# Retention feeding a softplus feed-forward layer: one 128x256 matmul per head in place of three 128x128, with the parts added in PSUM by VectorE

## The chip, the cores and the metric

The kernel runs on one core of a Trainium2 chip. The metric is device time in microseconds of one execution, as a median over several runs. TensorE does matrix products into PSUM, VectorE (DVE), ScalarE (ACT) and GpSimd (POOL) do elementwise work, and SyncE (SP) issues DMAs.

## The reference, cut to what matters

```python
gamma = 1.0 - 2.0 ** (-5.0 - np.arange(H))          # one decay per head; B, H, S, D = 4, 8, 768, 64
for t in range(S):
    state = gamma[None, :, None, None] * state + np.einsum('bhd,bhe->bhde', k[:, :, t], v[:, :, t])
    y[:, :, t] = scale * np.einsum('bhd,bhde->bhe', q[:, :, t], state)
...
x = y.transpose(0, 2, 1, 3).reshape(B * S, H * D)   # 3072 tokens of 512
h = x @ w_in                                        # 512 -> 2048, weights come as 64-bit floats
g = np.maximum(h, 0.0) + np.log1p(np.exp(-np.abs(h)))
return (g @ w_out).astype(np.float32)               # 2048 -> 512
```

## The kernel before, in words

The first layer is computed in chunks of 128 positions. A unit is one chunk of one batch entry and half of the heads (4 heads, in two pairs), so there are 24 x 2 = 48 units. Within a unit the output of a head is the sum of two products: v with the masked scores of this chunk, and the state carried from earlier chunks with q. The first chunk of a batch entry has no state.

From unit 10 on (`WHOLE = 10`) products run in the format fp32r, with each operand split into a high and a low part, and three of the four partial products are made: high-high, high-low, low-high. The first ten units use whole fp32 operands.

A unit passes through the steps `load_unit`, `decay`, `operands` (transposes of k and q into the PSUM tile `tp`, then the split into `kq`, and `vhl` with v's high and low part), `scores` (two PSUM tiles `sc`, one for each pair of heads, then `ah` and `al`, the scores' high and low part, each masked by a select on GpSimd), `new_state` (PSUM tile `pp`) and `stack_and_outputs` (state `st`, then PSUM tile `yp`, then the high and low part `xh`, `xl` of the layer's output). These steps are placed on ticks, four ticks a unit: `PARTS = {-6: load_unit, -2: decay, 0: operands, 2: scores, 3: new_state, 5: stack_and_outputs}`. `tp`, `sc`, `pp` and `yp` share one pool of three PSUM banks, `ps_a`; the other five banks hold `hp` (two), `acc` (two) and a tile for converting weights (`wp`).

The second and third products run on blocks of 256 tokens, in 8 steps a block. A step is `hidden` (24 matmuls into `hp`), softplus (VectorE L293, ScalarE L294, VectorE L298, ScalarE L300 `gh`, GpSimd L302 `gl`) and, two steps later, `second` (12 matmuls into `acc`). In the steady part, one tick is traced after `hidden` and one after `second`. A block's first step is traced two ticks after the outputs that it reads. The final order of each engine's instructions is chosen before the run by a planner that works with a model of times, so neighbouring steps can mix; on the chip each engine keeps that order.

In `outputs`, a head of a unit takes three matmuls of v with the scores (L249 to L251) and, where there is a state, two with q's high and low part (L242, L243), each with 64 weight columns and 128 moving columns, all summed in the one PSUM tile `yp`. Then ScalarE makes `xh` (L255) and VectorE `xl` (L257).

The tile `w` (L85, converted weights) has a pool `wts` of two slots of its own; `o` (L326, results on the way out) has two slots in the pool `ffn`.

Of the kernel before, what the change touches and what calls it, by code (L numbers as in the profile page):

```python
# [10 lines left out]
F32 = mybir.dt.float32  # L11
F32R = mybir.dt.float32r
I64 = mybir.dt.int64
U32 = mybir.dt.uint32
AF = mybir.ActivationFunctionType
ALU = mybir.AluOpType

P = 128
C = 128
# [3 lines left out]
WHOLE = 10  # L23
# [7 lines left out]
def decay_attention_then_softplus_ffn(ctx: ExitStack, tc: tile.TileContext, q, k, v, w_in, w_out, qtab, vtab, gtab, out):  # L31
    nc = tc.nc
    B, H, S, D = q.shape
    DM, DF = w_in.shape
# [4 lines left out]
    HH = H // 2  # L39
    NJ = HH // 2  # L40
# [2 lines left out]
    const = ctx.enter_context(tc.tile_pool(name="const", bufs=1))  # L43
    attn = ctx.enter_context(tc.tile_pool(name="attn", bufs=1))
    ffn = ctx.enter_context(tc.tile_pool(name="ffn", bufs=2))
    wts = ctx.enter_context(tc.tile_pool(name="wts", bufs=2))
    ps_h = ctx.enter_context(tc.tile_pool(name="ps_h", bufs=2, space=bass.MemoryType.PSUM))
    ps_o = ctx.enter_context(tc.tile_pool(name="ps_o", bufs=1, space=bass.MemoryType.PSUM))
    ps_w = ctx.enter_context(tc.tile_pool(name="ps_w", bufs=1, space=bass.MemoryType.PSUM))
    ps_a = ctx.enter_context(tc.tile_pool(name="ps_a", bufs=3, space=bass.MemoryType.PSUM))  # L50
# [23 lines left out]
    def convert_weights(f):  # L74

        n = ND * P
        converts[f] = []
        for nm, bits, to in zip(("win", "wout"), raw.pop(f), (win, wout)):
            words = bits.bitcast(U32).rearrange("p (n t) -> p n t", t=2)
            low, high = words[:, :, 0], words[:, :, 1]  # L80

            nc.scalar.activation(high.bitcast(F32), high.bitcast(F32), AF.Copy, scale=2.0**-112)

            wp = ps_w.tile([P, n], U32, name="wp")
            w = wts.tile([P, n], U32, name="w")  # L85

            nc.scalar.activation(wp, low, AF.Copy, scale=(1 - SLACK) * 2.0**-29, bias=7.5 * SLACK - 0.5)
            nc.vector.scalar_tensor_tensor(wp, high, 0x80000000, wp, op0=ALU.bitwise_and, op1=ALU.bitwise_or)
            nc.vector.scalar_tensor_tensor(w, high, 3, wp, op0=ALU.logical_shift_left, op1=ALU.bitwise_or)
            to[f] = const.tile([P, 2, n], F32R, name=f"{nm}hl", tag=f"{nm}{f}")  # L90
            converts[f].append(nc.scalar.copy(to[f][:, 0], w.bitcast(F32)).ins)
            nc.gpsimd.tensor_tensor(to[f][:, 1], w.bitcast(F32), to[f][:, 0].bitcast(F32), op=ALU.subtract)
# [4 lines left out]
    lo, up = slice(0, D), slice(D, P)  # L97
# [58 lines left out]
    def scores(n):  # L156
        kq = live[n][0]
        if n < WHOLE:
            kw, qw = kq
            parts = [attn.tile([P, HH, C], F32, name="ah")]  # L160
            sc = ps_a.tile([P, HH, C], F32, name="sc", tag="a")
            for h in range(HH):
                nc.tensor.matmul(sc[:, h, :], lhsT=kw[:, h // 2, :], rhs=qw[:, h % 2, h // 2, :], start=True, stop=True)
            nc.scalar.copy(parts[0], sc)
        else:
            parts = [attn.tile([P, HH, C], F32R, name=nm) for nm in ("ah", "al")]
            for j in range(NJ):

                sc = ps_a.tile([P, 2, 2, C], F32, name="sc", tag="a")
                for par in range(2):  # L170
                    nc.tensor.matmul(sc[:, par], lhsT=kq[:, 0, par, j, :], rhs=kq[:, 1:, par, j, :], start=True, stop=True)  # L171
                hi, low = (t[:, 2 * j:2 * j + 2, :] for t in parts)
                nc.scalar.copy(hi, sc[:, :, 0, :])
                nc.vector.tensor_tensor(low, sc[:, :, 0, :], hi.bitcast(F32), op=ALU.subtract)
                nc.vector.tensor_tensor(low, sc[:, :, 1, :], low.bitcast(F32), op=ALU.add)
        for t in parts:
            nc.gpsimd.affine_select(
                t, t.bitcast(F32), pattern=[[0, HH], [1, C]], compare_op=ALU.is_ge, fill=0.0, base=0, channel_multiplier=-1
            )
        live[n] += parts  # L180

# [45 lines left out]
    def outputs(n):  # L227
        b, c, hf = units[n]
        kq, *rest, st = live.pop(n)
        i, off = divmod((n // 2) * C, T)  # L230
        if i not in xs:
            xs[i] = [ffn.tile([P, ND, T], F32R, name=nm) for nm in ("xh", "xl")]
        xh, xl = xs[i]
        yp = ps_a.tile([D, 2, NJ, C], F32, name="yp", tag="a")
        for j in range(NJ):
            for par in range(2):
                h = 2 * j + par
                o = yp[:, par, j, :]
                if c and n < WHOLE:
                    nc.tensor.matmul(o, lhsT=st[:, j, :], rhs=kq[1][:, par, j, :], start=True, stop=False)  # L240
                elif c:
                    nc.tensor.matmul(o, lhsT=st[:, par, j, :], rhs=kq[:, 1, par, j, :], start=True, stop=False)  # L242
                    nc.tensor.matmul(o, lhsT=st[:, par, j, :], rhs=kq[:, 2, par, j, :], start=False, stop=False)  # L243
                if n < WHOLE:
                    kn, vn, a = rest
                    nc.tensor.matmul(o, lhsT=vn[:, h, :], rhs=a[:, h, :], start=c == 0, stop=True)  # L246
                else:
                    vhl, kh, kl, ah, al = rest
                    nc.tensor.matmul(o, lhsT=vhl[:, h, 0, :], rhs=ah[:, h, :], start=c == 0, stop=False)  # L249
                    nc.tensor.matmul(o, lhsT=vhl[:, h, 0, :], rhs=al[:, h, :], start=False, stop=False)  # L250
                    nc.tensor.matmul(o, lhsT=vhl[:, h, 1, :], rhs=ah[:, h, :], start=False, stop=True)  # L251
        g = hf * NJ
        to = [(par, x[rows, g:g + NJ, off:off + C]) for x in (xh, xl) for par, rows in ((0, lo), (1, up))]
        for par, hi in to[:2]:
            nc.scalar.copy(hi, yp[:, par])  # L255
        for (par, low), (_, hi) in zip(to[2:], to[:2]):
            nc.vector.tensor_tensor(low, yp[:, par], hi.bitcast(F32), op=ALU.subtract)  # L257

    def stack_and_outputs(n):
        stack_state(n)  # L260
# [1 line left out]


    PARTS = {-6: load_unit, -2: decay, 0: operands, 2: scores, 3: new_state, 5: stack_and_outputs}
    FIRST_TICK = min(PARTS)
    PERIOD = 4
# [38 lines left out]
    def second(s):  # L305
        i, p = steps[s]
        gh, gl = gs.pop(s)
        begins = s == 0 or steps[s - 1][0] != i
        ends = s + 1 == len(steps) or steps[s + 1][0] != i
        if begins:  # L310
            acc[i] = [ps_o.tile([P, DM], F32, name=f"acc{t}") for t in range(NT)]
        for k in range(2):
            wt = wout[2 * p + k]
            for t in range(NT):
                ts = slice(t * P, (t + 1) * P)
                nc.tensor.matmul(acc[i][t], lhsT=gh[:, k, ts], rhs=wt[:, 0], start=begins and k == 0, stop=False)  # L316
                nc.tensor.matmul(acc[i][t], lhsT=gh[:, k, ts], rhs=wt[:, 1], start=False, stop=False)  # L317
                nc.tensor.matmul(acc[i][t], lhsT=gl[:, k, ts], rhs=wt[:, 0], start=False, stop=ends and k == 1)  # L318
        if not ends:
            return  # L320
        for t in range(NT):
            if p < NP - 1:
                part[i, t] = ffn.tile([P, DM], F32, name="part")
                (nc.scalar.copy if t % 2 else nc.vector.tensor_copy)(part[i, t], acc[i][t])
                continue
            o = ffn.tile([P, DM], F32, name="o")  # L326
            if (i, t) in part:
                nc.vector.tensor_tensor(o, acc[i][t], part.pop((i, t)), op=ALU.add)
            else:
                (nc.scalar.copy if t % 2 else nc.vector.tensor_copy)(o, acc[i][t])  # L330
            nc.sync.dma_start(out[i * T + t * P:i * T + (t + 1) * P, :], o)
# [13 lines left out]
    def convert_to(n):  # L345
        nonlocal loaded, converted
        while converted < min(NF, n):
            convert_weights(converted)
            converted += 1
            if loaded < NF:  # L350
                load_weights(loaded)
                loaded += 1
# [30 lines left out]
    for a, b in zip(starts, starts[1:]):  # L383
        i = steps[b][0]
        if i == 2:
            a = b - TURN
# [4 lines left out]
    def stages(s, until):  # L391

        nonlocal done
        ok = lambda t: 0 <= t < len(steps)
        if ok(s):
            hidden(s)
            softplus_1(s)
            softplus_2(s)
        until = max(until, done)
        half = (done + until + 1) // 2  # L400
        while done < half:
            tick(done)
            done += 1
        if ok(s - LAG):
            second(s - LAG)
        while done < until:
            tick(done)
            done += 1
# [37 lines left out]
```

## Time and profile before

| | |
|---|---|
| median of 3 runs | 700.75 us (699.87 to 701.68) |
| the profiled execution | 700.03 us, span 698.2 us |
| busy: TensorE, its weight loads | 684.4, 621.3 us |
| busy: VectorE, ScalarE, GpSimd | 433.2, 372.1, 281.4 us |
| granted TensorE clock | 1.00 |

The span is the time from the first to the last instruction. Busy times of matmuls overlap one another, as matmuls are pipelined, so the cost of one is better read from the distance between starts. A row of a group gives line, engine, operation, tiles (written <- read), shape and count, then busy us and mean ns of one, then the engine's idle time ahead of it and what ended that.

### The profile page before, as it was taken

The page shows a single profiled execution, that of the slowest core. Times are in us where ns is not written, and L with a number is a line of the kernel's source. Part 1 is how long each engine was busy: PE and PEld are TensorE (multiplying, and loading weights), DVE is VectorE, ACT ScalarE, POOL GpSimd, SP SyncE. Part 2 cuts the span into 40 slices and gives each one's busy share as a digit, 9 for nine tenths or more (in the row PEclk, how much of TensorE's full clock was granted, in tenths as well). Part 3 has the DMA queues.
Part 4 walks back from the last instruction along what each step waited for, and adds up shares of the span by engine and source line. Part 5 has one row for each costly group of instructions (what it writes and reads, how often), then busy time and mean ns, then how long its engine had stood idle before and what let it go on. Part 6 is the DMA issues. An engine that isn't in the chain of part 4 may idle for free.

```text
span 698.2 us, 13537 instructions
## 1 busy us (share of the span) xinstructions
PE 684.4 (98%) x5056; PEld 621.3 (89%) x5056; DVE 433.2 (62%) x893; ACT 372.1 (53%) x835; POOL 281.4 (40%) x324
## 2 busy tenths in 40 slices
PE   6899999999999999999999999999999999999997
PEld 4688889899999999999999999999999999999996
DVE  4676785557666766557667666647766676544221
ACT  6988885446556546445555555445555544543221
POOL 5676667334343342343334333433433333222221
PEclk9999999999999999999999999999999999999999
DMA  9976650122112112111111111211211110000000
GB/s 266 287 201 173 192 159 1 31 61 69 31 23 69 31 25 61 31 31 54 39 23 37 49 38 24 61 37 25 62 24 39 54 31 16 31 1 1 31 1 30
DMA packets 90752, 42.82 MB, mean 61 GB/s; under 512 B 77376, under 2 KB 85568, under 8 KB 90688
## 3 DMA queue, kind: packets, MB, share of 16 engines
q1 hardware_dynamic: 90240, 41.96, 22.2%
q8 instruction: 40, 0.66, 0.4%
q14 instruction: 24, 0.20, 0.1%
q10 hardware_dynamic: 448, 0.01, 0.0%
HBM read 35.66 MB, written 6.29 MB: 60 GB/s over the span
## 4 chain that ended last, share of the span: by engine, by line
PE 96%; ACT 1%; issue 0%; DVE 0%; ACTq 0%
PE hp L286 14%; PE hp L287 13%; PE hp L288 13%; PE acc L316 13%; PE acc L317 13%; PE acc L318 13%; PE sc L171 3%; PE tp L125 1%; PE tp L127 1%; PE pp L195 1%; PE yp L250 1%; PE yp L251 1%; PE yp L249 1%; PE yp L246 1%; PE yp L240 1%; PE yp L243 1%
## 5 line engine op out<-in xcount | busy, mean ns | idle before, releaser
L286 PE MATMUL hp<-xh,winhl 128*128 128x256 f32 x768 | 221.4, 289 | 0.4 <-ACT xh L255 0.4
L288 PE MATMUL hp<-xh,winhl 128*128 128x256 f32 x768 | 217.9, 284 | 0.0
L287 PE MATMUL hp<-xl,winhl 128*128 128x256 f32 x768 | 217.6, 283 | 0.0
L302 POOL TENSOR_TENSOR gl<-sp,gh 128x512 fp32r<-128x512 f32 x96 | 125.4, 1306 | 149.3 <-ACT gh L300 86.7
L316 PE MATMUL acc<-wouthl,gh 128*128 128x512 f32 x384 | 154.3, 402 | 0.0
L317 PE MATMUL acc<-wouthl,gh 128*128 128x512 f32 x384 | 150.4, 392 | 0.0
L318 PE MATMUL acc<-wouthl,gl 128*128 128x512 f32 x384 | 149.1, 390 | 0.0
L286 PEld LDWEIGHTS hp<-xh,winhl 128*128 128x128 f32 x768 | 146.5, 191 | 2.8 <-issue 0.5
L287 PEld LDWEIGHTS hp<-xl,winhl 128*128 128x128 f32 x768 | 147.0, 191 | 1.6 <-issue 0.5
L288 PEld LDWEIGHTS hp<-xh,winhl 128*128 128x128 f32 x768 | 146.8, 191 | 0.6 <-issue 0.3
L293 DVE TENSOR_SCALAR sp<-hp 128x512 uint32<-128x512 uint32 x96 | 66.1, 690 | 70.6 <-PE hp L288 61.0
L300 ACT CAST gh<-sp 128x512 fp32r<-128x512 f32 x96 | 59.5, 620 | 74.1 <-PE acc L317 57.4
L117 POOL TENSOR_TENSOR qn<-qn,qtabs 128x256 f32<-128x256 f32 x48 | 29.4, 613 | 151.1 <-DMA qn<-in_q_dram 125.0
L294 ACT ACTIVATE sp<-sp 128x512 f32<-128x512 f32 x96 | 60.9, 634 | 49.0 <-DVE sp L293 48.7
L318 PEld LDWEIGHTS acc<-wouthl,gl 128*128 128x128 f32 x384 | 71.9, 188 | 15.6
L316 PEld LDWEIGHTS acc<-wouthl,gh 128*128 128x128 f32 x384 | 72.4, 189 | 12.5 <-issue 0.5
L317 PEld LDWEIGHTS acc<-wouthl,gh 128*128 128x128 f32 x384 | 72.5, 189 | 11.4
L298 DVE SCALAR_TENSOR_TENSOR sp<-hp,sp 128x512 f32<-128x512 f32 x96 | 65.9, 687 | 12.8 <-ACT sp L294 11.6
L142 DVE TENSOR_TENSOR kq<-tp,kq 64x256 fp32r<-64x256 f32 x76 | 32.1, 422 | 67.0 <-ACT kq L140 65.8
L139 ACT CAST kq<-tp 64x512 fp32r<-64x512 f32 x76 | 44.1, 581 | 40.0 <-PE tp L127 38.8
L255 ACT CAST xh<-yp 64x256 fp32r<-64x256 f32 x96 | 35.1, 366 | 51.0 <-PE yp L251 44.5
L257 DVE TENSOR_TENSOR xl<-yp,xh 64x256 fp32r<-64x256 f32 x96 | 39.9, 416 | 33.7 <-ACT xh L255 32.7
(85 smaller groups left out, 1082.6 us busy)
## 6 DMA issues: line engine op xcount, KB each, us to landing
win<-in_moe_w_in_dram SPq DMA_DIRECT2D x16, 512.0 KB, 4.5
wout<-in_moe_w_out_dram SPq DMA_DIRECT2D x16, 512.0 KB, 4.4
kn<-in_k_dram SPq DMA_DIRECT2D x48, 128.0 KB, 2.3
qn<-in_q_dram SPq DMA_DIRECT2D x48, 128.0 KB, 2.8
vn<-in_v_dram SPq DMA_DIRECT2D x48, 128.0 KB, 2.2
out_dram<-o SPq DMA_DIRECT2D x24, 256.0 KB, 2.1
gtab_sb<-in_gtab_dram ACTq DMA_DIRECT2D x2, 2.0 KB, 3.8
qtabs<-in_qtab_dram ACTq DMA_DIRECT2D x1, 4.0 KB, 2.4
```

What stands on the lines that cost most here:

```text
L139: nc.scalar.copy(kq[own, :2, par], tp[own])
L286: nc.tensor.matmul(hp[:, k], lhsT=wt[:, 0, d, :], rhs=xh[:, d, :], start=d == 0, stop=False)
L287: nc.tensor.matmul(hp[:, k], lhsT=wt[:, 0, d, :], rhs=xl[:, d, :], start=False, stop=False)
L288: nc.tensor.matmul(hp[:, k], lhsT=wt[:, 1, d, :], rhs=xh[:, d, :], start=False, stop=d == ND - 1)
L293: nc.vector.tensor_scalar(sp.bitcast(U32), hps[s].bitcast(U32), 0x80000000, None, op0=ALU.bitwise_or)
L294: nc.scalar.activation(sp, sp, AF.Softplus)
L298: nc.vector.scalar_tensor_tensor(g, hps.pop(s), 0.0, g, op0=ALU.max, op1=ALU.add)
L300: nc.scalar.copy(gh, g)
L302: nc.gpsimd.tensor_tensor(gl, sps.pop(s), gh.bitcast(F32), op=ALU.subtract)
L316: nc.tensor.matmul(acc[i][t], lhsT=gh[:, k, ts], rhs=wt[:, 0], start=begins and k == 0, stop=False)
L317: nc.tensor.matmul(acc[i][t], lhsT=gh[:, k, ts], rhs=wt[:, 1], start=False, stop=False)
L318: nc.tensor.matmul(acc[i][t], lhsT=gl[:, k, ts], rhs=wt[:, 0], start=False, stop=ends and k == 1)
```

## The change

The scores' two parts go into one tile `ahl` with the parts side by side for each head, masked by one select over both. In `outputs`, v's high and low part (128 weight columns) are multiplied with both parts of the scores (256 moving columns) in one matmul a head. It writes four fields: partitions 0 to 63 hold v-high with scores-high and, beside it, v-high with scores-low; partitions 64 to 127 hold v-low with scores-high and v-low with scores-low, and the last is not read. The matmuls with the state add into the first field. Then, for each of the two heads-in-pair positions, ScalarE copies the v-low field to partitions 0 to 63 of an SBUF tile `cross`, VectorE adds the v-high-scores-low field to it, and VectorE adds `cross` into the first field in PSUM. `xh` and `xl` are made from that field as before. `yp` is now one PSUM bank for each of the two positions, so two a unit. The first ten units keep their form. The pool `wts` goes; `w` shares the two slots of `o`.

```diff
-    wts = ctx.enter_context(tc.tile_pool(name="wts", bufs=2))
...
-            w = wts.tile([P, n], U32, name="w")
+            w = ffn.tile([P, n], U32, name="w", tag="o")
...
-            parts = [attn.tile([P, HH, C], F32R, name=nm) for nm in ("ah", "al")]
+            ahl = attn.tile([P, HH, 2, C], F32R, name="ahl", tag="ahl")
+            parts = [ahl]
...
-                hi, low = (t[:, 2 * j:2 * j + 2, :] for t in parts)
+                hi, low = (ahl[:, 2 * j:2 * j + 2, t, :] for t in range(2))
...
+            t = t if n < WHOLE else t.rearrange("p h t c -> p (h t) c")
             nc.gpsimd.affine_select(
-                t, t.bitcast(F32), pattern=[[0, HH], [1, C]], compare_op=ALU.is_ge, fill=0.0, base=0, channel_multiplier=-1
+                t, t.bitcast(F32), pattern=[[0, t.shape[1]], [1, C]], compare_op=ALU.is_ge, fill=0.0, base=0, channel_multiplier=-1
             )
...
-                    vhl, kh, kl, ah, al = rest
-                    nc.tensor.matmul(o, lhsT=vhl[:, h, 0, :], rhs=ah[:, h, :], start=c == 0, stop=False)
-                    nc.tensor.matmul(o, lhsT=vhl[:, h, 0, :], rhs=al[:, h, :], start=False, stop=False)
-                    nc.tensor.matmul(o, lhsT=vhl[:, h, 1, :], rhs=ah[:, h, :], start=False, stop=True)
...
+            vhl, kh, kl, ahl = rest
+            ys = []
             for par in range(2):
+                yp = ps_a.tile([P, NJ, 2, C], F32, name="yp", tag="a")
+                for j in range(NJ):
+                    h = 2 * j + par
+                    nc.tensor.matmul(yp[:, j], lhsT=vhl[:, h], rhs=ahl[:, h], start=True, stop=True)
+                    if c:
+                        o = yp[lo, j, 0, :]
+                        nc.tensor.matmul(o, lhsT=st[:, par, j, :], rhs=kq[:, 1, par, j, :], start=False, stop=False, skip_group_check=True)
+                        nc.tensor.matmul(o, lhsT=st[:, par, j, :], rhs=kq[:, 2, par, j, :], start=False, stop=True, skip_group_check=True)
+                cross = attn.tile([D, NJ, C], F32, name="cross", bufs=2)
+                nc.scalar.copy(cross, yp[up, :, 0, :])
+                nc.vector.tensor_tensor(cross, yp[lo, :, 1, :], cross, op=ALU.add)
+                nc.vector.tensor_tensor(yp[lo, :, 0, :], yp[lo, :, 0, :], cross, op=ALU.add)
+                ys.append(yp[lo, :, 0, :])
+        for y, (hi, low) in zip(ys, to):
+            nc.scalar.copy(hi, y)
+        for y, (hi, low) in zip(ys, to):
+            nc.vector.tensor_tensor(low, y, hi.bitcast(F32), op=ALU.subtract)
```

More of the change, by code (lines that the diff above doesn't have):

```diff
@@ L159, in scores @@
             kw, qw = kq
-            parts = [attn.tile([P, HH, C], F32, name="ah")]
+            parts = [attn.tile([P, HH, C], F32, name="ah", tag="ahl")]
             sc = ps_a.tile([P, HH, C], F32, name="sc", tag="a")
@@ L233, in outputs @@
         xh, xl = xs[i]
-        yp = ps_a.tile([D, 2, NJ, C], F32, name="yp", tag="a")
-        for j in range(NJ):
-            for par in range(2):
[L237 to L247, printed above, removed]
-                    vhl, kh, kl, ah, al = rest
-                    nc.tensor.matmul(o, lhsT=vhl[:, h, 0, :], rhs=ah[:, h, :], start=c == 0, stop=False)
-                    nc.tensor.matmul(o, lhsT=vhl[:, h, 0, :], rhs=al[:, h, :], start=False, stop=False)
-                    nc.tensor.matmul(o, lhsT=vhl[:, h, 1, :], rhs=ah[:, h, :], start=False, stop=True)
@@ L252, in outputs @@
[L252 to L257, printed above, removed]
+        g = hf * NJ
+        to = [[x[rows, g:g + NJ, off:off + C] for x in (xh, xl)] for rows in (lo, up)]
+        if n < WHOLE:
+            kn, vn, a = rest
+            yp = ps_a.tile([D, 2, NJ, C], F32, name="yp", tag="a")
+            for j in range(NJ):
+                for par in range(2):
+                    o = yp[:, par, j, :]
+                    if c:
+                        nc.tensor.matmul(o, lhsT=st[:, j, :], rhs=kq[1][:, par, j, :], start=True, stop=False)
+                    nc.tensor.matmul(o, lhsT=vn[:, 2 * j + par, :], rhs=a[:, 2 * j + par, :], start=c == 0, stop=True)
+            ys = [yp[:, par] for par in range(2)]
+        else:
+            vhl, kh, kl, ahl = rest
+            ys = []
+            for par in range(2):
+                yp = ps_a.tile([P, NJ, 2, C], F32, name="yp", tag="a")
+                for j in range(NJ):
+                    h = 2 * j + par
+                    nc.tensor.matmul(yp[:, j], lhsT=vhl[:, h], rhs=ahl[:, h], start=True, stop=True)
+                    if c:
+                        o = yp[lo, j, 0, :]
[6 more added lines that the diff above has]
+                ys.append(yp[lo, :, 0, :])
@@ L325, in second @@
                 continue
-            o = ffn.tile([P, DM], F32, name="o")
+            o = ffn.tile([P, DM], F32, name="o", tag="o")
             if (i, t) in part:
```

## The prediction

> **What bounds the kernel now.** I read the page's busy times first, then the windows by stage, then the waits of TensorE, and last the order in time around one group of v-times-score products.
>
> ```profile
> PE 684.4 (98%) x5056; PEld 621.3 (89%) x5056; DVE 433.2 (62%) x893; ACT 372.1 (53%) x835; POOL 281.4 (40%) x324
> ```
>
> ```profile
> 28.00:136.00 108.00, 108.00 (x748) 94.58 (x747) 74.01 (x126) 81.96 (x168) 69.27 (x69) 1.00 0.49 139
> ...
> 150.00:640.00 490.00, 490.00 (x3746) 451.72 (x3746) 321.83 (x693) 249.68 (x587) 178.35 (x208) 1.00 0.14 37
> ```
>
> The columns of the window rows are the stretch, its length, busy time of PE, PEld, DVE, ACT and POOL with counts, the granted clock, and the DMA share and rate. TensorE is busy in every one of the 490 us of the stage that the change touches, at a granted clock of 1.00, and VectorE in 322 of them (66%). The waits of TensorE, asked for the whole span, are a handful, all small and nearly all in the opening part; the last of them on the new code's path is this one:
>
> ```profile
> PE hp L286 <- ACT xh L255: 0.4, 1, 0.4
> ```
>
> So time comes off only where TensorE's own stream gets shorter, and goes on where TensorE gets a wait that it does not have now. A busy TensorE says little on what one matmul costs, since records overlap (0.22 us long, one every 0.06 us). I therefore price matmuls by the distance from one start to the next. One unit without a carried state (first column start, second duration):
>
> ```profile
> 333.25 0.39 PE L316 MATMUL acc<-wouthl,gh 128*128 128x512 f32 x1
> 333.48 0.39 PE L317 MATMUL acc<-wouthl,gh 128*128 128x512 f32 x1
> ...
> 333.93 0.22 PE L249 MATMUL yp<-ah,vhl 128*64 128x128 f32 x1
> 333.99 0.22 PE L250 MATMUL yp<-al,vhl 128*64 128x128 f32 x1
> ...
> 334.59 0.22 PE L251 MATMUL yp<-ah,vhl 128*64 128x128 f32 x1
> 334.65 0.33 PE L286 MATMUL hp<-xh,winhl 128*128 128x256 f32 x1
> 334.82 0.28 PE L287 MATMUL hp<-xl,winhl 128*128 128x256 f32 x1
> 334.94 0.28 PE L288 MATMUL hp<-xh,winhl 128*128 128x256 f32 x1
> ```
>
> Twelve yp matmuls of 128 moving columns take 334.65 - 333.93 = 0.72, so 0.06 each. An hp matmul of 256 columns takes 0.12, but the first after the yp group takes 0.17. An acc matmul of 512 takes 0.23. The weight loads tell where the extra 0.05 comes from:
>
> ```profile
> 334.53 0.13 PEld L251 LDWEIGHTS yp<-ah,vhl 128*64 128x64 f32 x1
> 334.59 0.19 PEld L286 LDWEIGHTS hp<-xh,winhl 128*128 128x128 f32 x1
> 334.70 0.19 PEld L287 LDWEIGHTS hp<-xl,winhl 128*128 128x128 f32 x1
> ...
> 340.86 0.14 PEld L195 LDWEIGHTS pp<-vhl,kh 128*64 128x64 f32 x1
> 340.92 0.14 PEld L196 LDWEIGHTS pp<-vhl,kl 128*64 128x64 f32 x1
> ```
>
> A load begins when the matmul ahead of its own begins (L286's load at 334.59 with L251's matmul at 334.59), so one load is ahead, not more. The load of 128 weight columns holds the next one off for 0.11, a load of 64 for 0.06. The pitch is thus the longer of two things: streaming this matmul's columns, or loading the next one's weights. After a yp matmul (0.06 of streaming) a load of 128 columns (0.11) shows as 0.05 lost.
>
> **The change part by part.** The form with high and low parts is used from unit 10 on:
>
> ```profile
> L249 PE MATMUL yp<-ah,vhl 128*64 128x128 f32 x152 | 33.2, 223 | 0.0
> L242 PE MATMUL yp<-kq,st 128*64 128x128 f32 x128 | 28.4, 222 | 0.0
> L171 PE MATMUL sc<-kq 128*128 128x256 f32 x152 | 25.3, 283 | 0.0
> ```
>
> 152 heads are 38 units; 128 of them have a state, so 32 units have one and 6 have none.
>
> *TensorE, the 6 units without a state.* Removed: 12 matmuls at 0.06, and the 0.05 on the following hp: 0.77. Added: 4 matmuls of 256 columns with 128 weight columns, the shape of L171, whose tile below shows four in 352.00 - 351.51 = 0.49, 0.12 each: 0.48. The next hp's load hides under 0.12. Gain 0.29 x 6 = 1.7 us.
>
> *TensorE, the 32 units with a state.* Removed: 20 x 0.06 + 0.05 = 1.25. After: for each head one wide matmul (0.12, the load of 64 columns hides under it), the first state matmul (0.06), the second state matmul, behind which a load of 128 columns must run (0.11, not 0.06). That is 0.29 a head, 1.16 a unit. Gain 0.09 x 32 = 2.9 us. Here nearly all of the three-to-one saving goes: the head has 3 matmuls for 5, but the wide weights are loaded behind a matmul too short to hide them.
>
> TensorE's sum is -4.6 us. Its bounds: at the good end every load hides, then each unit saves 0.29 and the sum is -11.0. At the bad end a wide load behind a state matmul costs what it costs behind pp's 64-column matmul, where the next hp takes 0.20 in place of 0.12:
>
> ```profile
> 341.21 0.19 PE L196 MATMUL pp<-vhl,kl 128*64 128x64 f32 x1
> 341.24 0.36 PE L286 MATMUL hp<-xh,winhl 128*128 128x256 f32 x1
> 341.44 0.28 PE L287 MATMUL hp<-xl,winhl 128*128 128x256 f32 x1
> ```
>
> Then a unit with state takes 4 x (0.12 + 0.06 + 0.06 + 0.08) = 1.28, loses 0.03, and the sum is +1.0 - 1.7 = -0.7. I take -4.6, since L286 behind L251 has the very shapes: 128 moving columns, then 128 weight columns.
>
> The Trainium skill speaks against this change too: TensorE: Matmul & The Clock Gate, section LDWEIGHTS, gives a load as weight columns over 1.2, so 107 ns for 128. By it a state unit takes 4 x (0.12 + 0.06 + 0.107) = 1.15 and the sum would be -4.9; the rows agree with it.
>
> *ScalarE and VectorE.* Added per unit, for each of two halves: a ScalarE copy of 64x256 out of PSUM (cross), a VectorE add of PSUM and SBUF into SBUF, and a VectorE add of PSUM and SBUF into PSUM. Prices by these rows:
>
> ```profile
> L140 ACT CAST kq<-tp 64x256 fp32r<-64x256 f32 x76 | 27.9, 367 | 0.9
> L202 DVE TENSOR_TENSOR td<-pp,td 64x256 f32<-64x256 f32 x32 | 13.3, 414 | 16.7 <-PE pp L196 15.7 <-PE pp L191 0.9
> L88 DVE SCALAR_TENSOR_TENSOR wp<-win,wp 128x512 uint32<-128x512 uint32 x16 | 11.1, 694 | 10.1 <-ACT wp L87 10.1
> L89 DVE SCALAR_TENSOR_TENSOR w<-win,wp 128x512 uint32<-128x512 uint32 x16 | 11.0, 685 | 0.9
> ```
>
> L88 writes PSUM and L89 SBUF, 694 against 685 ns, so an output in PSUM costs nothing to speak of. ScalarE gets 2 x 0.37 x 38 = 28 us, VectorE 4 x 0.414 x 38 = 63 us, to 496 of some 695 us, and about 380 of the 490 us stage (78%). Neither becomes the bound as a whole. Their cost is in latency only; what hides it is below.
>
> ```profile
> 347.39 0.22 PE L242 MATMUL yp<-kq,st 128*64 128x128 f32 x1
> ...
> 348.13 0.43 DVE L143 TENSOR_TENSOR kq<-tp,kq 64x256 fp32r<-64x256 f32 x1
> 348.59 0.69 DVE L298 SCALAR_TENSOR_TENSOR sp<-hp,sp 128x512 f32<-128x512 f32 x1
> 350.36 0.85 DVE L257 TENSOR_TENSOR xl<-yp,xh 64x256 fp32r<-64x256 f32 x2 [1.08 <-ACT xh L255]
> 351.23 0.43 DVE L147 TENSOR_TENSOR vhl<-vn,vhl 128x256 fp32r<-128x256 f32 x1
> 351.79 0.69 DVE L293 TENSOR_SCALAR sp<-hp 128x512 uint32<-128x512 uint32 x1
> ...
> 351.51 0.64 PE L171 MATMUL sc<-kq 128*128 128x256 f32 x4
> 352.00 0.40 PE L316 MATMUL acc<-wouthl,gh 128*128 128x512 f32 x1
> ```
>
> This unit's yp group runs from 347.39 for 20 x 0.06, to 348.59. VectorE has 1.08 idle ahead of xl; the adds are 1.66. So L293 starts some 0.6 later, and with it softplus, whose gh is read two steps later: covered. xl ends up to 1 us later than 351.20. A block's first hidden matmuls come behind 24 hp (2.9), 4 sc (0.5), 12 acc (2.7) and the pp matmuls after the last unit of the block: over 6 us against a chain of under 4. Covered.
>
> *PSUM banks.* Each unit now takes two banks of the pool of three for yp, not one. tp holds the third until L143 ends (348.56). The first sc tile can have tp's bank; the second needs the first yp tile's, free when its xl has been made. That is the one new wait on TensorE, and the acc matmuls are queued behind it. VectorE's shortest way there is 348.56 + 0.69 + 4 x 0.414 + 0.42 = 351.33, with the gaps of some 0.02 between instructions about 351.45; the second sc tile is wanted at 351.51 + 0.24 - 0.09 = 351.66. So it passes by 0.2, at nothing. Bounds: nothing, or 0.3 a unit (rival below). Below nothing it cannot be, as TensorE does not wait there now.
>
> *POOL.* Two selects of 128x512 become one of 128x1024, behind the later of the two parts. It costs at most twice 0.634 = 1.27:
>
> ```profile
> L177 POOL TENSOR_SCALAR_AFFINE_SELECT al<-al x38: 629/634/819, 132.6 to 636.5; 128x512 fp32r<-128x512 f32 x38
> ```
>
> The yp matmuls that read it come three ticks after sc, with at least 12 acc matmuls (2.7) or 24 hp (2.9) between ticks, and POOL is busy 178 of 490 us: nothing.
>
> *w in the slots of o.* Two slots as before, and the last w is written at 117.9 us, the first o at 140.4: nothing.
>
> ```profile
> L89 DVE SCALAR_TENSOR_TENSOR w<-wout,wp x16: 678/687/691, 12.5 to 117.9; 128x512 uint32<-128x512 uint32 x16
> ...
> L330 DVE COPY o<-acc x11: 678/680/692, 140.4 to 693.4; 128x512 f32<-128x512 f32 x11
> ```
>
> No DMA is added, removed or moved past anything.
>
> *The last unit* has no ticks behind it:
>
> ```profile
> 644.42 0.85 DVE L257 TENSOR_TENSOR xl<-yp,xh 64x256 fp32r<-64x256 f32 x2 [2.57 <-ACT xh L255]
> ...
> 646.96 0.28 PE L286 MATMUL hp<-xh,winhl 128*128 128x256 f32 x1
> ```
>
> Its xl ends at 645.27, VectorE idle ahead of it. One half's cross and two adds (0.37 + 2 x 0.41), which stay in its chain, take it to near 646.5, still ahead of the hp matmuls that read it, which come behind 12 acc. Nothing.
>
> The sum is -4.6. The profiled execution took 700.03 (span 698.2), 0.7 below the median of 700.75; against the median it is 696.1.
>
> **The rivals.**
>
> *A: as summed.* TensorE saves 2.2 to 7, no wait: 694 to 698.5 with 696.1 likeliest.
>
> *B: all loads hide.* 700.75 - 11.0 = 689.7. It needs a wide load that begins two matmuls ahead; against it, L286's load begins no earlier than L251's matmul. The Trainium skill, same page, section The mechanism, says that TensorE's queue pulls a load ahead of matmuls in flight where it goes to the background weights; by it this rival would come out; the trace shows one matmul ahead and no more.
>
> *C: part is given back.* The second sc tile waits about 0.1 a unit, 38 x 0.1 = 3.8: 699.9, no change to be told. For it: a margin of only 0.2. Against it: instructions are put in an order beforehand, and acc matmuls can be put ahead of sc.
>
> *D: the wait on the yp bank decides; slower.* If VectorE takes vhl (0.43) ahead of xl, the first yp tile comes free at 351.9 and TensorE stands 0.3 in each unit: 38 x 0.3 = 11.4, and 700.75 - 4.6 + 11.4 = 707.5. It decides from 4.6 / 38 = 0.12 a unit on. For it: vhl belongs to the unit's operands, traced ahead of the outputs. Against it: vhl comes last now although VectorE idles 1.08 ahead of xl.
>
> **How the numbers follow.** A 0.56, B 0.08, C 0.20, D 0.16. Within 0.3% (2.1 us, about what can be told from no change) lies C alone. Faster 0.64, same 0.20, slower 0.16. The range 691 to 703.5 leaves out B and most of D.
>
> **What would show it.** TensorE, by starts: 0.12 for the wide matmul, 0.06 and 0.11 for the two state matmuls; wide loads beginning with the second state matmul. Units without state: four at 0.12. VectorE near 496 us and ScalarE near 400. TensorE's waits: no row of sc on xl. Wrong it is if sc L171's second tile waits for VectorE by over 0.1 a unit, or if state matmuls are 0.06 throughout.

## The result and the profile after

The changed kernel takes 724.1 us as a median against 700.6 for the kernel before: ratio 1.033, interval 1.028 to 1.038. The forecast was 696.1, range 691.0 to 703.5. The four executions lie between 720.5 and 726.8; the profiled one is the longest of them, 726.77 us (span 725.0, so 26.8 more than before's 698.2).

The page's busy times, and the window of the middle stage (same columns as before: stretch, length, PE, PEld, DVE, ACT, POOL with counts, granted clock, DMA):

```profile
PE 694.9 (96%) x4752; PEld 631.6 (87%) x4752; DVE 472.8 (65%) x1045; ACT 398.1 (55%) x911; POOL 273.6 (38%) x286
```

```profile
150.00:640.00 490.00, 473.50 (x3300) 437.35 (x3299) 340.92 (x798) 262.79 (x631) 164.35 (x167) 0.98 0.14 37
```

Two things are new. TensorE, busy for all 490 us before, now stands still for 16.5 of them. And the granted clock, 1.00 before, is 0.98. The list of TensorE's waits names two causes that the kernel before did not have:

```profile
PE sc L172 <- DVE kq L142: 8.6, 9, 1.4
PE hp L298 <- DVE sp L310: 8.2, 10, 0.9
```

The columns are total us, times, longest. Nine waits for `kq` and ten for softplus's second VectorE instruction (one of them, 0.3 us, in the opening part): one pair for each block of the middle part, since a block takes about 58 us there and the stage is some 490. None is on `xl`, the tile whose lateness the prediction's rivals turned on.

The saving in TensorE's own stream is there, to the price. One yp group with a state, TensorE and its weight loads:

```profile
391.92 0.28 PE L256 MATMUL yp<-ahl,vhl 128*128 128x256 f32 x1
392.04 0.22 PE L259 MATMUL yp<-kq,st 128*64 128x128 f32 x1
392.10 0.22 PE L260 MATMUL yp<-kq,st 128*64 128x128 f32 x1
392.16 0.33 PE L256 MATMUL yp<-ahl,vhl 128*128 128x256 f32 x1
392.33 0.22 PE L259 MATMUL yp<-kq,st 128*64 128x128 f32 x1
392.39 0.22 PE L260 MATMUL yp<-kq,st 128*64 128x128 f32 x1
392.45 0.33 PE L256 MATMUL yp<-ahl,vhl 128*128 128x256 f32 x1
```

```profile
392.39 0.19 PEld L256 LDWEIGHTS yp<-ahl,vhl 128*128 128x128 f32 x1
392.50 0.14 PEld L259 LDWEIGHTS yp<-kq,st 128*64 128x64 f32 x1
```

The first wide matmul takes 0.12 to the next start, the state matmuls 0.06 each, and the second wide one 0.17. The extra 0.05 comes from the load of the wide weights. The load rows show it for the third wide matmul (392.45): its load begins with the state matmul ahead of it (L260 at 392.39) and holds the next load off for 0.11, to 392.50. That is 0.29 a head, as summed, so the forecast saving of 4.6 us in the stream stands. The other 31 us, by which the profiled execution is longer in spite of it, must lie in what TensorE waits for and in its clock.

**Where one pair of waits comes from.** The stretch around 392 us, in order of time (start, duration, engine, instruction; idle time ahead of it in brackets):

```profile
386.42 0.40 PE L172 MATMUL sc<-kq 128*128 128x256 f32 x2
388.88 0.41 DVE L176 TENSOR_TENSOR ahl<-sc,ahl 128x256 fp32r<-128x256 f32 x1
389.45 0.38 PE L124 MATMUL tp<-ident,kn 128*128 128x128 f32 x2
391.66 0.37 ACT L139 CAST kq<-tp 64x256 fp32r<-64x256 f32 x1
391.93 0.63 ACT L306 ACTIVATE sp<-sp 128x512 f32<-128x512 f32 x1
392.06 0.42 DVE L141 TENSOR_TENSOR kq<-tp,kq 64x256 fp32r<-64x256 f32 x1 [1.36 <-ACT kq L139]
393.36 0.43 DVE L142 TENSOR_TENSOR kq<-tp,kq 64x256 fp32r<-64x256 f32 x1
393.82 0.69 DVE L305 TENSOR_SCALAR sp<-hp 128x512 uint32<-128x512 uint32 x1
393.94 0.47 PE L172 MATMUL sc<-kq 128*128 128x256 f32 x2 [0.74 <-DVE kq L142]
394.54 0.69 DVE L310 SCALAR_TENSOR_TENSOR sp<-hp,sp 128x512 f32<-128x512 f32 x1
395.29 0.39 PE L298 MATMUL hp<-xh,winhl 128*128 128x256 f32 x1 [0.88 <-DVE sp L310]
```

Read it backwards. hp at 395.29 needs the hp bank that L310 frees. L310 is late since VectorE had to do four kq subtracts (L141 and L142, twice each) and L305 first. sc at 393.94 waits for the last of these subtracts. Before, kq had 12 acc, the yp and 24 hp matmuls of cover between `tp` (the row below, from the kernel before) and `sc` at 351.51, 7.3 us; here `sc` comes 4.5 us behind `tp`, right behind the yp matmuls, with no acc between. The missing acc matmuls are the mark of these places. In the middle part the changed kernel has nine units with no acc between `tp` and the first `sc` tile and 4.5 us from one to the other, and all nine wait; its other units have at least 12 acc there and 6.7 us or more, and none waits for kq. In all the other runs below, too, the first `sc` tile waits for kq only where no acc stands between (17 or 18 hp matmuls, 3.3 to 4.5 us).

```profile
344.19 0.38 PE L125 MATMUL tp<-ident,kn 128*128 128x128 f32 x2
```

In the changed kernel `tp` starts at 389.45, just after L176 (388.88 to 389.29) has read the previous unit's second `sc` tile for the last time. That tile's matmuls had come late in their turn (386.42).

**The clock.** In seven stretches of 3.4 us the granted clock was half. The first and the last of seven windows:

```profile
222.50:225.90 3.40, 3.40 (x19) 3.40 (x18) 2.47 (x7) 1.49 (x4) 2.12 (x3) 0.50 0.17 39
...
628.60:632.00 3.40, 3.32 (x15) 3.32 (x16) 2.94 (x9) 1.95 (x5) 1.95 (x2) 0.51 0.00 0
```

```profile
396.60 0.42 PE L299 MATMUL hp<-xl,winhl 128*128 128x256 f32 x1
396.82 0.42 PE L300 MATMUL hp<-xh,winhl 128*128 128x256 f32 x1
```

hp matmuls are 0.22 apart there, not 0.12. Each stretch begins within 1.4 us of the end of a pair of waits (seven of the nine pairs) and costs about 3.41 x (1 - 0.12 / 0.22) = 1.55 us, all seven 11. An eighth, at 24.5 us in the opening part, belongs to no such pair; the profiled execution before has none there, so it adds 1.5. The nine pairs of waits cost 2.0 to 2.6 each by start distances (0.9 to 1.5 at `sc`, 1.0 at hp), 18 to 20 us. With -4.6 that makes +26 to +28, against +26.8 measured. The four executions had granted clocks of 0.981 to 0.991, which is some eight to four half-clock stretches each: the median, 724.1, has fewer than the profiled execution.

### The profile page after: what moved, and what is told of

It reads as the page before. It is cut to its first block, busy times and chain, and to the rows that moved or that the text cites. A ratio compares the mean times of both kernels' runs of the same rounds, so it can differ in the third digit from the quotient of the medians.

```text
span 725.0 us, 13053 instructions
## 1 busy us (share of the span) xinstructions
PE 694.9 (96%) x4752; PEld 631.6 (87%) x4752; DVE 472.8 (65%) x1045; ACT 398.1 (55%) x911; POOL 273.6 (38%) x286
## 4 chain that ended last, share of the span: by engine, by line
PE 89%; DVE 4%; ACT 3%; issue 1%; DMA 0%; POOL 0%; POOLq 0%; DVEq 0%; ACTq 0%
PE hp L298 13%; PE acc L328 12%; PE hp L299 12%; PE hp L300 12%; PE acc L329 12%; PE acc L330 12%; PE yp L256 3%; PE sc L172 2%; PE tp L124 1%; PE pp L197 1%; PE tp L126 1%; PE yp L246 1%; PE sc L162 1%; PE yp L245 1%; ACT kq L138 1%; DVE sp L310 1%
## 5 line engine op out<-in xcount | busy, mean ns | idle before, releaser
L298 PE MATMUL hp<-xh,winhl 128*128 128x256 f32 x768 | 222.3, 292 | 8.6 <-DVE sp L310 8.2
L299 PE MATMUL hp<-xl,winhl 128*128 128x256 f32 x768 | 224.5, 292 | 0.0
L300 PE MATMUL hp<-xh,winhl 128*128 128x256 f32 x768 | 222.6, 290 | 0.0
L314 POOL TENSOR_TENSOR gl<-sp,gh 128x512 fp32r<-128x512 f32 x96 | 123.9, 1291 | 215.7 <-ACT gh L312 180.0
L298 PEld LDWEIGHTS hp<-xh,winhl 128*128 128x128 f32 x768 | 150.5, 197 | 14.9 <-DVE sp L310 9.7
L299 PEld LDWEIGHTS hp<-xl,winhl 128*128 128x128 f32 x768 | 151.3, 197 | 3.5 <-issue 0.5
L300 PEld LDWEIGHTS hp<-xh,winhl 128*128 128x128 f32 x768 | 151.5, 197 | 0.5 <-issue 0.2
L305 DVE TENSOR_SCALAR sp<-hp 128x512 uint32<-128x512 uint32 x96 | 65.8, 687 | 56.7 <-PE hp L300 53.3
L310 DVE SCALAR_TENSOR_TENSOR sp<-hp,sp 128x512 f32<-128x512 f32 x96 | 66.1, 688 | 11.0 <-ACT sp L306 9.1
L179 POOL TENSOR_SCALAR_AFFINE_SELECT ahl<-ahl 128x1024 fp32r<-128x1024 f32 x38 | 42.2, 1111 | 63.3 <-DVE ahl L176 50.4
L117 POOL TENSOR_TENSOR vn<-vn,vtabs 128x256 f32<-128x256 f32 x48 | 29.5, 615 | 87.2 <-DMA vn<-in_v_dram 47.2
L263 DVE TENSOR_TENSOR cross<-yp,cross 64x256 f32<-64x256 f32 x76 | 30.6, 409 | 43.5 <-ACT cross L262 43.4
L175 DVE TENSOR_TENSOR ahl<-sc,ahl 128x256 fp32r<-128x256 f32 x76 | 31.2, 411 | 36.0 <-ACT ahl L174 35.9
```

The lines of the kernel that those rows point to most:

```text
L179: nc.gpsimd.affine_select(t, t.bitcast(F32), pattern=[[0, t.shape[1]], [1, C]], compare_op=ALU.is_ge, fill=0.0, base=0, channel_multiplier=-1)
L298: nc.tensor.matmul(hp[:, k], lhsT=wt[:, 0, d, :], rhs=xh[:, d, :], start=d == 0, stop=False)
L299: nc.tensor.matmul(hp[:, k], lhsT=wt[:, 0, d, :], rhs=xl[:, d, :], start=False, stop=False)
L300: nc.tensor.matmul(hp[:, k], lhsT=wt[:, 1, d, :], rhs=xh[:, d, :], start=False, stop=d == ND - 1)
L305: nc.vector.tensor_scalar(sp.bitcast(U32), hps[s].bitcast(U32), 0x80000000, None, op0=ALU.bitwise_or)
L310: nc.vector.scalar_tensor_tensor(g, hps.pop(s), 0.0, g, op0=ALU.max, op1=ALU.add)
```

## The experiments

The question was which part of the change upsets the order: the second PSUM bank for yp, or the instructions added to VectorE and ScalarE. The planner makes a new order for each kernel, so all runs compare orders that the planner chose, too.

**A fourth bank.** In both kernels:

```diff
-    ps_w = ctx.enter_context(tc.tile_pool(name="ps_w", bufs=1, space=bass.MemoryType.PSUM))
-    ps_a = ... bufs=3
+    ps_a = ... bufs=4
-            wp = ps_w.tile([P, n], U32, name="wp")
+            wp = ps_a.tile([P, n], U32, name="wp", tag="a")
```

> The changed kernel, but the weight-conversion tile wp is taken from the same PSUM pool as tp, sc, pp and yp, and that pool has 4 banks in place of 3 (8 in all, as before). Theory 1 (banks: two of three banks held by yp push the planned order of sc and hidden behind the new chain, and the waits of about 2 us in each of 9 blocks, with the half-clock windows that follow, come from it): waits go, about 696 us (TensorE's shorter stream, -4.6). Theory 2 (VectorE: the four added instructions a unit, in VectorE's fixed order, hold back kq and softplus whatever the banks): about 720, waits on L142 and L310 remain.

> The kernel before with the same 4-bank pool, as the control. Theory 1 and theory 2 both: 699 to 701, as TensorE has no wait that a bank would remove; what it gains below 700 would be due to the banks alone and has to be taken off the other kernel's gain.

Measured: 701.97 with the change (ratio to the kernel before 1.0008, 0.9995 to 1.0022), 702.06 without (1.0015, 1.0005 to 1.0025). The pairs of waits are gone but for one place near 163 us, so 22 of the 23.5 us come back with a bank. Neither expected number was met. In the changed kernel the place near 163 us keeps 2.5 us of waits and has a half-clock stretch of 6.8 us (some 3 us lost) behind it, together more than TensorE's shorter stream saves. And in the opening part, where `wp` now competes with the attention tiles, TensorE stands still for 4 us in both kernels, as its busy time in the window shows for the changed one (108.00 there before):

```profile
28.00:136.00 108.00, 104.26 (x721) 91.48 (x720) 71.66 (x127) 81.58 (x169) 69.42 (x69) 1.00 0.51 147
```

**The second bank alone**, with the old products: `yp` is allocated once for each of the two positions, and the loops over `par` and `j` change places.

> The kernel before, with its 128x128 products and no added VectorE work, but with yp as one PSUM bank for each of the two head positions, so two a unit out of three (matmuls in the order of positions). Theory 1: waits appear as in the changed kernel, 712 to 724. Theory 2: no change, 700 to 703.

Measured: 700.86 (1.0001, 0.9990 to 1.0013). Two of three banks for yp cost nothing by themselves. The theory that the banks alone do it is wrong.

**The added work alone**, with one yp bank:

```diff
+        if n >= WHOLE:
+            for par in range(2):
+                cross = attn.tile([D, NJ, C], F32, name="cross", bufs=2)
+                nc.scalar.copy(cross, yp[:, par])
+                nc.vector.tensor_tensor(cross, yp[:, par], cross, op=ALU.subtract)
+                nc.vector.tensor_tensor(yp[:, par], yp[:, par], cross, op=ALU.add)
```

> The kernel before, one yp bank, with the same added instructions per unit: for each half a ScalarE copy of yp into cross, a VectorE subtract of cross from yp into cross (zero) and a VectorE add of cross into yp in PSUM, so that the result stays; w shares the slots of o as in the changed kernel. Theory 1: banks suffice, 700 to 703. Theory 2: VectorE's load brings the waits without the second bank, 712 to 728.

Measured: 702.37 (1.0018, 1.0007 to 1.0028). The four VectorE instructions a unit cost 1.3 us by themselves, although the one yp bank is now held long: in one unit its matmuls end at 352.5 and its last xl at 361.6 us, with no wait of TensorE there. The theory that VectorE's load alone does it is wrong too.

**The change without the added work**: the copy into `cross` and both adds left out.

> The changed kernel without the ScalarE copy and the two VectorE adds of each half (the two small fields are computed but not added to the result). Banks as in the changed kernel. Theory 1: banks are held for a shorter time but still two of three: 702 to 715. Theory 2: about 696, no waits on VectorE.

Measured: 695.35 (0.9925, 0.9910 to 0.9940), by the ratio 5.3 us faster than the kernel before. TensorE waits once, 0.6 us, in its middle part. The profiled executions, both at full clock throughout, have spans of 693.6 and 698.2, so 4.6 apart. This is what the prediction's first term is worth when the added work is left out.

So neither part costs much alone, and together they cost 23.5 us: two banks held through a chain that is a copy and two adds longer for each half. The following runs try that. The two parts together around the old products were not run, so whether the wide product itself has a share is open.

**One add fewer.**

```diff
-                nc.vector.tensor_tensor(yp[lo, :, 0, :], yp[lo, :, 0, :], cross, op=ALU.add)
```

> The changed kernel without the second add of each half (the sum in cross is made and not added to the result), so VectorE has two added instructions a unit in place of four and xl follows the yp matmuls at once. Theory 1a (the wait grows with the time that both yp banks are held): between 695 (no adds) and 724, about 705 to 715. Theory 1b (what decides is whether the planner still places both sc tiles of a unit together; in this kernel's order they are apart in nearly all units, as in the changed kernel): 715 to 724.

Measured: 697.55 (0.9959, 0.9947 to 0.9972); both theories missed. One pair of waits is left, in place of nine, so the loss does not grow in step with the work added. The edit does more than take away two VectorE adds a unit (0.8 us in some 14): xh and xl need no longer wait for `cross`. Which of the two counts can't be told from this run. That the two `sc` tiles of a unit lie apart is not by itself the cause: here too they do in all units of the middle part. What differs is what stands ahead of them. From 150 to 645 us an `sc` tile comes straight behind yp in 31 places in the changed kernel and in two here, and the one pair of waits is at one of these.

**The first half finished ahead of the second**: `xh` and `xl` of the first half traced right behind its adds.

```diff
                 ys.append(yp[lo, :, 0, :])
+                hi, low = to[par]
+                nc.scalar.copy(hi, ys[par])
+                nc.vector.tensor_tensor(low, ys[par], hi.bitcast(F32), op=ALU.subtract)
```

> The changed kernel with xh and xl of the first half traced right behind that half's two adds, ahead of the second half's, so that the first yp bank comes free about two adds and a copy (1.2 us) sooner; three banks as in the changed kernel. Theory 1: the second sc tile is planned earlier; 696 to 710. Theory 2: no VectorE work goes, about 724.

Measured: 724.06 (1.032, 1.029 to 1.035). The waits are the same to the tenth, 8.6 and 8.2 us. The planner gives VectorE the same order as in the changed kernel, for all its 1045 instructions, with both halves' adds ahead of the first xl, so the edit moves nothing and tests nothing. The rows of the changed kernel:

```profile
367.00 1.04 DVE L146 TENSOR_TENSOR vhl<-vn,vhl 128x256 fp32r<-128x256 f32 x1
367.97 0.41 DVE L264 TENSOR_TENSOR yp<-yp,cross 64x256 f32<-64x256 f32 x1
368.96 0.41 DVE L264 TENSOR_TENSOR yp<-yp,cross 64x256 f32<-64x256 f32 x1
369.30 0.40 DVE L269 TENSOR_TENSOR xl<-yp,xh 64x256 fp32r<-64x256 f32 x1
370.66 0.42 DVE L269 TENSOR_TENSOR xl<-yp,xh 64x256 fp32r<-64x256 f32 x1
372.50 0.40 PE L172 MATMUL sc<-kq 128*128 128x256 f32 x2
```

The yp matmuls of this unit end at 366.5. The last xl ends at 371.1, 4.6 us later (it was 2.7 before), and the unit's second sc tile comes at 372.5.

**The fourth bank without the opening part's loss**: the second yp tile of a unit goes into the bank of `wp`, which is idle from 118 us on.

```diff
-                yp = ps_a.tile([P, NJ, 2, C], F32, name="yp", tag="a")
+                yp = (ps_w if par else ps_a).tile([P, NJ, 2, C], F32, name="yp", tag="wp" if par else "a")
```

> The changed kernel, with the second yp tile of each unit placed in the PSUM bank of wp (whose last use, at 118 us, is before the first wide product). The opening part keeps its banks, and the later part has four for tp, sc, pp and yp. Theory 1 (two banks of three held through the longer chain): 695 to 697, the whole of TensorE's saving. Theory 2 (VectorE's load itself): over 705.

Measured: 699.02 (0.9968, 0.9957 to 0.9980), faster than the kernel before but not the whole saving. The two sc tiles of a unit are together again, right behind a full row of hp matmuls, as before the change:

```profile
203.54 0.28 PE L300 MATMUL hp<-xh,winhl 128*128 128x256 f32 x1
203.66 0.64 PE L172 MATMUL sc<-kq 128*128 128x256 f32 x4
204.14 0.40 PE L328 MATMUL acc<-wouthl,gh 128*128 128x512 f32 x1
```

What is left is one passage near 162 us, with waits of 2.5 us and one half-clock stretch behind them (some 1.6 us):

```profile
PE hp L298 <- DVE sp L310: 1.6, 1, 1.6
PE sc L172 <- DVE kq L142: 0.9, 2, 0.5
```

**More room between outputs and their block**: `AHEAD` 4 in place of 2, first with three banks.

> The changed kernel, three banks, with AHEAD = 4 in place of 2: the attention steps are traced two ticks earlier against the blocks that read them. If the wait of each block comes because a block's outputs are too late for it, it shrinks: 700 to 712. If it comes from the order of tp, yp and sc within a unit (sc right behind yp, kq not ready), it stays: 718 to 726.

Measured: 709.52 (1.013, 1.011 to 1.015), at the slow end of the first expectation. The waits on kq are gone: nine units still have no acc between `tp` and `sc`, but 34 hp matmuls, and 5.0 to 5.7 us. Those on L310 stay once a block (nine of the eleven):

```profile
PE hp L298 <- DVE sp L310: 11.1, 11, 1.9
```

Of the changed kernel's eight half-clock stretches one is left, so some 11 of the 17.2 us between the two profiled spans (725.0 and 707.8) are the clock's. Most of the loss that is left stands as waits.

> The kernel with the second yp tile in the bank of wp, and AHEAD = 4. If the wait near 160 us is a late output of the second layer's input: 695 to 697. If it is the crowding of VectorE and ScalarE there: 698 to 702.

> The kernel before with AHEAD = 4 alone, the control for the last version. TensorE waits nowhere in its middle part, so an earlier place of the attention steps can take nothing away there: 700 to 703, up to 2 us more by the opening part. If it falls to 698 or below, that version's gain over the kernel before is AHEAD's and not the wide product's.

> The kernel with the second yp tile in the bank of wp, and TURN = 6 in place of 5, which moves the crowded passage near 160 us, where that kernel waits 2.5 us and then has one half-clock window. If the passage loosens: 695 to 697. Otherwise 698 to 701.

With the yp tile in the bank of `wp`, `AHEAD = 4` gives 696.76 (0.9946, 0.9929 to 0.9963). Its control, the kernel before with `AHEAD = 4`, gives 701.75 (1.0009, 0.9998 to 1.0020), so the gain is not that of `AHEAD` alone: it comes with the wide product. `TURN = 6` gives 705.21 (1.006, 1.004 to 1.008): the passage near 160 us is free, but the opening part now stands still and falls to half clock:

```profile
28.00:136.00 108.00, 100.29 (x674) 87.90 (x673) 70.22 (x123) 78.99 (x163) 65.48 (x66) 0.95 0.48 139
136.00:640.00 504.00, 504.00 (x3594) 467.05 (x3594) 377.07 (x854) 283.69 (x678) 176.38 (x177) 1.00 0.15 37
```

The best version is the changed kernel with the second yp tile in the bank of `wp` and `AHEAD = 4`, 0.5% faster than the kernel before. TensorE is busy throughout its middle stage again, with VectorE at 75%:

```profile
150.00:640.00 490.00, 489.95 (x3496) 453.40 (x3495) 368.88 (x835) 275.94 (x661) 172.78 (x173) 1.00 0.14 36
```

## Why the prediction was wrong

**TensorE's stream: right.** -4.6 was forecast; the start distances bear out its prices, and the run without the added work gives -5.3 by the ratio and -4.6 between the profiled executions. The price of a wide load behind a narrow matmul, 0.05, was read off the hp matmul behind the old yp group and came out the same. Rival B, all loads hidden, is excluded by the rows.

**ScalarE, VectorE and POOL by themselves: right.** 0.41 us an add and 0.37 a copy were forecast, and the adds alone cost 1.3 us. VectorE's busy time came to 473 us, not 496: the adds are there at their price (61 us), but other instructions took less, above all the `kl` subtracts (L153 before, L152 after), 437 ns on average in place of 970. Why they did was not tried. One select of 128x1024 took 1.11, under the bound of 1.27:

```profile
L179 POOL TENSOR_SCALAR_AFFINE_SELECT ahl<-ahl 128x1024 fp32r<-128x1024 f32 x38 | 42.2, 1111 | 63.3 <-DVE ahl L176 50.4 <-ACT st L222 11.8 <-ACT kq L138 1.1
```

**The step that failed is "PSUM banks".** It found the right resource and set it at nothing, with a margin of 0.2 us in one unit's chain. It assumed that the old order of all engines would stay and that only one wait could be new, of sc on xl. The order did not stay. In the one place where the wait was looked for there is none. In its place the unit's steps are planned otherwise: sc tiles apart and straight behind yp, `tp` behind the last read of an sc tile, and once in each block `tp`, yp and `sc` with no acc between them, where kq and softplus are both late. That is where TensorE waits, 18 to 20 us in all. Its paragraph on ScalarE and VectorE failed with it: it called softplus covered because gh is read two steps later, and left out that L310 also frees the hp bank that TensorE writes next, which is 7.9 of the 16.5 us that TensorE stands still in the middle stage. Rival D had the right resource and the right sign, but another form (0.3 in each unit, 707.5), and 0.16 of the chance. Its condition came true in the unit shown: VectorE takes vhl (L146 at 367.00) ahead of xl. But no wait on xl came of it.

**The second thing left out is the clock.** The prediction priced a wait at its length. Here 18 to 20 us of waits brought some 11 us more at half clock.

**What stays open.** That both parts are needed is shown (one bank with the adds, two banks without them, and two banks with half of the adds are none of them over 1.3 us slower than the kernel before), and that a fourth bank removes the waits is shown. That the units' chain through three banks becomes too long for the pace of the blocks, and the planner makes up for it at one point of each block, is what the order looks like, and is argued only. Runs with a fixed order were not made, and the added work on two banks around the old products was not tried.

## What to carry to other kernels

In a kernel whose order is planned ahead, the cover of a longer chain is not what lies beside it in the old trace: count, for each pool, how long every buffer is held in one period, and where a change holds more of its buffers through a longer chain, allow for another order of all engines, with a loss of several per cent in the range. In the new trace, look first for places where work that used to cover a chain is missing. Give the longer-held tile a buffer that is idle in that stage before the engine is blamed. When TensorE is the bound, price a pause by its length and by the half-clock stretch that can follow.

## What the runs showed of the hardware

In these traces the half clock follows idle time within a fixed window, not any one gap. The half-clock stretches are 3.41 us long and lie a whole number of 3.41 us apart within a run. In one place two follow each other, 6.8 us. Laying that grid over each run and adding up TensorE's idle time from the start distances, all 18 half-clock stretches of the middle part, in the five runs that have any, begin after a window with some 1.8 us or more of idle time (half of the window is 1.71), and no window at full clock with 1.61 us or less is followed by one. A pause of 2.0 us in one piece (`AHEAD` 4 with three banks, from 331.6 us) was followed by none where the grid cut it in two. The Trainium skill, TensorE: Matmul & The Clock Gate, section Why this matters for your kernels, advises against gaps over about 3 us between matmuls; here two pauses of some 1 us each within one window were enough.
